# Four operations of the later phases moved: a v load to ScalarE's queue, a split unit by a slot, a weight table by a product, sums and split steps by one place

## The chip, the cores and the metric

One core of a Trainium2 chip runs the kernel. The metric is the device time of one execution in microseconds, the median over runs. TensorE (PE) multiplies, VectorE (DVE), ScalarE (ACT) and GpSimd (POOL) do elementwise work, and SyncE (SP) issues most DMAs; ScalarE and GpSimd can issue DMAs from their own queues as well. Each engine works through its instructions in the order in which the program gives them.

## What is computed

```python
# attention, per batch and head (4, 8, 768, 64), with 16 clusters
q_assign = argmax(normalized(q) @ normalized(centroids).T)      # and k_assign
scores = (q @ k.T) / 8, -1e9 where q_assign != k_assign
attn = softmax(scores);  y = attn @ v
# then, with the heads side by side: x is 3072 x 512
h = x @ w_in                     # 512 x 2048
g = h if h > 0 else exp(h) - 1
out = g @ w_out                  # 2048 x 512
```

## The kernel before

The kernel has three phases on one core, each a long stream for PE. All orders are written out by hand: an operation stands at the place in the program where it should come on its engine.

**Attention** runs in 32 slots, one per batch, half of the queries and pair of heads. A slot multiplies k by q for six key tiles (lines 540 and 553, the second is the cluster mask), ScalarE exponentiates each tile (line 576), and one slot later PE multiplies by v (line 596, `values`), ScalarE takes the result (line 610, `take_values`). In `told_and_values` v of slot n + 1 is asked for (`load_v`, line 195), in a buffer that the values of slot n - 1 have just left; in the slots of `second_of_pair` (3, 5, ..., 15) this stands behind the six key tiles, in the others ahead. q and k come in small pieces (line 181, sixteen loads for one half of the queries). Between the tiles the slots convert weights (lines 344 to 374, with a power step on ScalarE at line 354) and split pieces of w_in into rounded parts for the last phase: `split_here` asks for a unit's store (line 1026), `split_after` runs its two ScalarE operations at the end of the slot (lines 1019 and 1033), and the next slot's `split_here` stores the result (line 1043) and adds by a DMA of GpSimd (line 1044). The slots that may start a unit are `split_slots`.

**The first 1024 tokens** go through w_in (`first_pair`, line 1276) and then through w_out by a recursion in which seven products of half size replace eight, twice over. The outer seven (`UNITS`, M1 to M7) each have a quadrant or sum of w_out (a11, a12, a22, s1 to s4) and of g. The inner seven of a unit (`chain`, m1 to m7) need sums of that quadrant, its "table" (s2, s3, s4): `table_last` makes a22's (two ScalarE copies, line 997, and GpSimd's accumulating DMAs, line 999), `table_block` s4's in four VectorE steps (lines 930, 932, 935, 937), called one by one as `next(fourth)`. Tables are stored to DRAM (`keep_far`, line 914), and later groups of tokens fetch them back piece by piece (`fetch`, line 1079) into slots that come free. Within `chain`, ScalarE copies banks (lines 1534, 1571, 1592), VectorE adds (1578, 1595), makes the next unit's t1 to t4 (`t_step`, lines 1622 to 1628), and takes the quarters of the unit before into the output (`take`, line 1654). `taken` closes a unit: for M6 two sums of 128x512 on VectorE (line 1673), for M5 and M4 the stores of two output tiles each by SP (line 1682), for the others nothing. Output tiles of the second group of tokens use the places of the first, so their first sums must wait for those stores. `note` marks the places within a unit at which side work stands.

**The other 2048 tokens** go through w_in in two parts of 28 products (`k_phase`, lines 1345, 1393, 1355), with x split into three rounded parts (`x_split`: steps 0 and 2 on ScalarE at lines 1019 and 1139, steps 1 and 3 on VectorE at 1137 and 1141) at products given by `SPLIT_AT`, and after each part through w_out by two more runs of `chain`. After every product ScalarE copies its bank (line 1393), PE adds the third part on the copy, and VectorE adds to the result (line 1355).

Of the kernel before, what the change touches and what calls it, by code (L numbers as in the profile page):

```python
# [61 lines left out]
def main_path(ctx, tc, c, q, k, v, centroids, moe_w_in, moe_w_out, out):  # L62
# [131 lines left out]

    def load_v(n):
        b, _, pr = blocks[n]
        nc.sync.dma_start(
            v_raw[n % 2].rearrange("p h t d -> p h (t d)"),
            v[b, 2 * pr : 2 * pr + 2].rearrange("h (p t) d -> p h (t d)", t=NT),
        )  # L200
# [789 lines left out]
    def table_last(a, at, n):  # L990

        q11, q12, q21, q22 = (part_w(a, i, j) for i in range(2) for j in range(2))
        s3, s2, s4 = at
        minus = [(s2, q11)] if n == 0 else [(s3, s2), (s4, s2)]
        more = [(q21, q22), (s2, q21)] if n == 0 else [(s3, q22), (s4, q12)]
        for to, x in minus:
            nc.scalar.activation(to, x, Act.Copy, scale=-1.0)
        for to, x in more:
            nc.gpsimd.dma_start(to, x, accum_op=Alu.add)
        if n == 1:  # L1000
            parts = [("s3", s3), ("s2", s2), ("s4", s4)]
            here[a].update(parts)
            made.extend((flat_far(a, x), y) for x, y in parts)
# [44 lines left out]

    to_split = [(a, u) for a in ("a11", "a12", "a22", "s1") for u in range(4)]
    last_piece = {"a11": 1, "a12": 3, "a22": 7, "s1": 7}  # L1050
    split_slots = (9, 13, 15, 17, 21, 23, *range(3 * NB, 4 * NB))

    def split_here(n):
        while in_hand:
# [263 lines left out]
    def late_elu(step, n, e):  # L1318
        x = late_part(n)
        if n > 3:  # L1320
            x, e = in_columns(x), in_columns(e)
        relu_of_exp(step, x, e)

    def k_phase(part):

        pool = bank_pool("doubles")
        d = [pool.tile([P, 2, 512], F32, name=f"double{n}") for n in range(4)]
        bank_a, bank_b = [d[1], d[0]], [d[2], d[3]]
        c11, c21, c12, c22 = s_of
        into = (c21, c11, c21, c12, c21, c21, c12)  # L1330
        plus = (None, c21, c21, c21, c21, c21, c12)
        x11, x21, t2, t1, x12, _, x22 = k_operands(part)
        def minus(to, x, y):
            nc.vector.tensor_tensor(to, x, y, op=Alu.subtract)

        begin = 28 * part
        at = of_unit

        def times(n, bank, parts, first):
            i, u = divmod(n, 4)  # L1340
            w, x = w_ring[(begin + n) % 3], xh[(7 * part + i) % 2]
            for j in range(2):
                for ch in range(2):
                    for m in parts:
                        nc.tensor.matmul(  # L1345
                            bank[:, j],
                            lhsT=w[:, m, QS * ch + P * j : QS * ch + P * j + P],
                            rhs=x[m][:, ch],
                            start=first and ch == 0 and m == parts[0],
                            stop=ch == 1 and m == parts[-1],  # L1350
                            skip_group_check=True,
                        )

        def add(to, x, y):
            nc.vector.tensor_tensor(to, x, y, op=Alu.add)  # L1355

        on_act, on_dve = ({n: [] for n in range(29)} for _ in range(2))

        def plan(of, n, what, *args):
            of[n].append(lambda: what(*args))  # L1360

        for i in range(6):
            if i == 0 and part:
                continue
            q = 7 * part + i + 1
            for what, (of, n) in enumerate(zip((on_act, on_dve, on_act, on_dve), SPLIT_AT[i])):
                plan(of, n, x_split, q, what)
        for n, x in zip(
            ((0, 1, 3, 6), (0, 1, 2, 3))[part],
            ((t1, x12, x11), (t2, x22, t1), (x12, x22, x12), (x21, x21, t2)),  # L1370
        ):
            plan(on_dve, n, minus, *x)
        for c_, exps, ends in ((c11, (7, 7, 10, 14), (9, 11, 13, 15)), (c21, (23, 24, 26, 27), (25, 26, 27, 28))):
            for u in range(4):
                plan(on_act, exps[u], k_exp, at(c_, u), u)
                if ends[u] < 28:
                    plan(on_dve, ends[u], k_elu, at(c_, u), u)
        for u, n in ((0, 21), (3, 23)):
            plan(on_dve, n, add, at(c22, u), at(c22, u), at(c12, u))
        for t in ("t1", "t2"):  # L1380
            plan(on_dve, 24, t_step, 2 + 2 * part, 0, t, t_first)

        for n in range(29):
            if n < 28:
                i, u = divmod(n, 4)
                a, b = bank_a[n % 2], bank_b[n % 2]
                times(n, a, (0, 1), True)
                if begin + n + 3 < 56:
                    k_load(begin + n + 3, (0, 1))
            for what in on_act[n]:  # L1390
                what()
            if n < 28:
                nc.scalar.activation(at(into[0], u) if n < 2 else b, a, Act.Copy, scale=K_OF)  # L1393
            for what in on_dve[n]:
                what()
            if n > 0:
                m = n - 1
                i, u = divmod(m, 4)
                b, to = bank_b[m % 2], at(into[i], u)
                times(m, b, (2,), m < 2)  # L1400
                if begin + m + 3 < 56:
                    k_load(begin + m + 3, (2,))
                if m < 2:
                    add(to, b, to)
                elif plus[i] is None:
                    nc.scalar.copy(to, b)
                else:
                    add(to, b, at(plus[i], u))
                    if i == 4 and u in (1, 2):
                        add(at(c22, u), b, at(c12, u))  # L1410
                    elif i == 4:
                        nc.scalar.copy(at(c22, u), b)
            if part == 0 and 24 <= n < 28:
                if n == 24:
                    until[0] = len(streamed)
                    slots[:] = [xT[:, ch, GS * x : GS * x + GS] for x in (2, 3) for ch in range(KC)]
                fetch()
                fetch()
        k_elu(at(c21, 3), 3)
        for t in ("t3", "t4"):  # L1420
            t_step(2 + 2 * part, 0, t, t_first)

    SPLIT_AT = [(0, 2, 3, 4)]
    SPLIT_AT += [(4 * n, 4 * n, 4 * n + 1, m) for n, m in ((1, 5), (2, 10), (3, 14), (4, 17), (5, 22))]

    def first_elu(x, e):
        nc.vector.scalar_tensor_tensor(x, e, -1.0, x, op0=Alu.mult, op1=Alu.max)
# [1 line left out]
    class OutUnit:  # L1429
# [27 lines left out]
        def note(self, at):  # L1457
            k_, n = self.k_, self.n
            if k_ == 0:
                if (n, at) == (3, "m2"):  # L1460
                    next(first_table, None)
                if at in ("m2", "m7") and n in (3, 4):
                    g_step(k_, 5 - n, at == "m7")
                if (n, at) == (3, "m4"):
                    late_elu(2, 5, k_e[1])
                    table_last("a22", last, 1)
                elif (n, at) == (5, "m6"):
                    verdict_told()
                if (n, at) in ((4, "m4"), (5, "m6"), (5, "m2"), (5, "m7")):
                    next(fourth)  # L1470
                if (n, at) == (5, "m2"):
                    slots[:] = [*words_of, *thirds(x_sum)]
                    for _ in range(4):
                        fetch()
                elif (n, at) == (5, "m4"):
                    keep_far()
                    for _ in range(3):
                        fetch()
                elif (n, at) == (6, "m7"):
                    slots[:] = slots + beside[:3]  # L1480
                    for _ in range(3):
                        fetch()
                return
            if k_ == 1:
                ahead_of_k(n, at)
            for step, x in ELU_STEPS[1 if k_ == 1 else 2 + k_ % 2].get((n, at), ()):
                late_elu(step, x, dead_e[x % 2] if k_ == 1 else k_e[x % 2])
            if (n, at) in G_STEPS:
                g_step(k_, *G_STEPS[n, at])
            if k_ == 3 and (n, at) in SPLIT_AHEAD:  # L1490
                x_split(*SPLIT_AHEAD[n, at])
# [68 lines left out]
    def chain(units):  # L1560
# [5 lines left out]
        for i, u in enumerate(units):  # L1566
# [5 lines left out]
            if i > 0:  # L1572
                for q_ in (2, 3):
                    units[i - 1].take(q_)
                units[i - 1].taken()
            if nxt:
                nxt.t("t1")
            nc.vector.tensor_tensor(b2, b2, u.m5, op=Alu.add)
            if nxt:
                nxt.t("t2")  # L1580
            u.note("m6")
# [512 lines left out]
```

## Time and profile before

| | us |
|---|---|
| runs | 850.65, 851.0, 858.26 (median 851.0) |
| profiled execution | 852.49 |
| its span, first to last instruction | 850.7 |
| PE busy | 838.0 |
| VectorE busy | 756.3 |
| ScalarE busy | 509.6 |
| GpSimd busy | 120.6 |

In the profile a row of a timeline gives its start, its length, the engine and line, and in brackets how long the engine idled before it and what ended that idle time. A releaser is inferred; where the engine named was long done, another one, often a DMA, was the last.

### The profile page before, as it was taken

What the parts mean: (1) busy time and instruction counts of PE and PEld (TensorE: products, weight loads), DVE (VectorE), ACT (ScalarE), POOL (GpSimd) and SP (SyncE); (2) the same over time, 40 slices, a digit from 0 to 9 for tenths busy, and PEclk for the clock granted to TensorE, in tenths of its full rate; (3) what the DMA queues carried; (4) which work ended last, traced back from release to release, by engine and by line L of the source; (5) the groups of instructions that cost most, each with busy time, mean ns of one, the idle gap of its engine ahead of it and who ended that gap; (6) DMA issues with size and microseconds to landing.
All of it is one profiled execution on the core that took longest, in us unless ns stands there. A gap on an engine that the chain in (4) does not pass through costs nothing.

```text
span 850.7 us, 15122 instructions
## 1 busy us (share of the span) xinstructions
PE 838.0 (99%) x5584; PEld 585.7 (69%) x5584; DVE 756.3 (89%) x993; ACT 509.6 (60%) x827; POOL 120.6 (14%) x139
## 2 busy tenths in 40 slices
PE   9999999999999999999999999999999999999997
PEld 5444444444444444444698998888999988789997
DVE  7899999999997988987899887889999859899995
ACT  6887777887878875543722326765543266655521
POOL 0023131312224324121011000102000001020000
PEclk9999999999999999999999999999999999999999
DMA  8786796789659997899389968999867798847683
GB/s 176 162 211 185 161 229 162 184 187 232 149 140 278 323 262 204 252 269 299 100 164 239 305 209 288 288 292 323 253 212 227 214 292 289 285 133 236 206 239 117
DMA packets 184577, 190.91 MB, mean 224 GB/s; under 512 B 97584, under 2 KB 131376, under 8 KB 183472
## 3 DMA queue, kind: packets, MB, share of 16 engines
q1 hardware_dynamic: 174688, 163.32, 64.7%
q0 software_dynamic: 8688, 25.17, 14.5%
q10 hardware_dynamic: 1120, 1.38, 0.6%
q8 instruction: 46, 0.75, 0.4%
q14 instruction: 35, 0.29, 0.1%
HBM read 130.06 MB, written 51.38 MB: 213 GB/s over the span
## 4 chain that ended last, share of the span: by engine, by line
PE 83%; DVE 7%; DMA 4%; ACT 3%; issue 2%; SPq 0%; POOL 0%; ACTq 0%; DVEq 0%; POOLq 0%
PE bank L1099 28%; PE double L1345 15%; PE banks L1276 11%; PE banks L540 11%; PE o_bank L596 9%; PE banks L553 3%; PE d_bank L596 3%; PE d_bank L616 1%; DMA k_a<-spare 1%; DMA kq_g<-in_v_dram 1%; PE banks L454 1%; ACT p_out L576 1%; DMA ring<-k_s 1%; DVE sums_w L580 1%; DMA out_dram<-p_out 1%
## 5 line engine op out<-in xcount | busy, mean ns | idle before, releaser
L576 ACT ACTIVATE p_out<-banks 128x768 f32<-128x768 f32 x150 | 118.4, 813 | 9.2 <-PE banks L540 6.7
L596 PE MATMUL o_bank<-p_out,kq_g 128*64 128x384 f32 x600 | 102.3, 490 | 0.4 <-DMA kq_g<-in_v_dram 0.4
L596 PEld LDWEIGHTS o_bank<-p_out,kq_g 128*64 128x64 f32 x600 | 40.8, 137 | 59.6 <-issue 54.4
L1099 PE MATMUL bank<-xT 128*128 128x128 f32 x640 | 80.6, 275 | 0.0
L1393 ACT ACTIVATE double<-double 128x1024 f32<-128x1024 f32 x52 | 52.3, 1009 | 42.6 <-PE double L1345 26.4
L1099 PEld LDWEIGHTS bank<-xT 128*128 128x128 f32 x640 | 76.0, 192 | 0.0
L1145 POOL TENSOR_SCALAR k_e<-k_e 128x1024 f32<-128x1024 f32 x16 | 18.6, 1163 | 282.6 <-ACT k_e L1144 282.6
L1276 PE MATMUL banks<-xT,w_in 128*128 128x512 f32 x128 | 55.6, 594 | 0.0
L1355 DVE TENSOR_TENSOR kq_g<-double,kq_g 128x1024 f32<-128x1024 f32 x36 | 44.0, 1222 | 12.8 <-PE double L1345 10.3
L580 DVE TENSOR_TENSOR sums_w<-p_out 128x1536 f32<-128x1536 f32 x25 | 46.2, 1848 | 9.0 <-ACT p_out L576 8.9
L1571 ACT COPY bank<-bank 128x128 f32<-128x128 f32 x39 | 9.8, 251 | 67.9 <-PE bank L1099 67.9
L583 DVE TENSOR_TENSOR sums_w<-sums_w,p_out 128x1536 f32<-128x1536 f32 x25 | 44.3, 1772 | 1.8
L1276 PEld LDWEIGHTS banks<-xT,w_in 128*128 128x128 f32 x128 | 24.2, 190 | 30.9 <-issue 30.2
L1345 PE MATMUL double<-xh0h,ring 128*128 128x512 f32 x112 | 43.9, 392 | 0.3 <-ACT double L1393 0.2
L654 POOL TENSOR_TENSOR xT<-xT,sums_b 128x384 f32<-128x384 f32 x32 | 43.0, 1358 | 6.7 <-DMA sums_b<-xT 4.6
L1345 PE MATMUL double<-xh1h,ring 128*128 128x512 f32 x112 | 43.7, 390 | 0.0
L1345 PE MATMUL double<-xh0l,ring 128*128 128x512 f32 x112 | 43.6, 389 | 0.0
L1345 PE MATMUL double<-xh1l,ring 128*128 128x512 f32 x112 | 43.6, 389 | 0.0
L1099 PE MATMUL bank<-w_out,xT 128*128 128x128 f32 x288 | 38.4, 276 | 1.2 <-DVE xT L1622 1.2
L540 PE MATMUL banks<-x_sum,xT 64*128 64x384 f32 x192 | 38.2, 486 | 0.8 <-ACT p_out L576 0.7
L540 PE MATMUL banks<-kq_g 64*128 64x384 f32 x192 | 37.6, 483 | 0.8 <-ACT p_out L576 0.8
L540 PE MATMUL banks<-kq_g,xT 64*128 64x384 f32 x192 | 37.6, 483 | 0.0
(335 smaller groups left out, 2023.7 us busy)
## 6 DMA issues: line engine op xcount, KB each, us to landing
ring<-k_s SPq DMA_DIRECT2D x32, 512.0 KB, 4.7
xT<-far_s_s SPq DMA_DIRECT2D x63, 256.0 KB, 3.3
kq_g<-in_v_dram SPq DMA_DIRECT2D x32, 384.0 KB, 5.5
ring<-k_a SPq DMA_DIRECT2D x23, 512.0 KB, 4.9
xT<-far_s_q SPq DMA_DIRECT2D x38, 256.0 KB, 3.1
xT<-far_a_s SPq DMA_DIRECT2D x37, 256.0 KB, 3.2
ring<-k_s SPq DMA_DIRECT2D x32, 256.0 KB, 4.5
k_a<-w_in SPq DMA_DIRECT2D x24, 256.0 KB, 7.6
```

The source lines that it names most:

```text
L540: nc.tensor.matmul(s[:, e, :HS], lhsT=kT[b % 2][pr][rows, ts(kt, P)], rhs=qT[half][pr][rows], start=first, stop=not first,)
L553: nc.tensor.matmul(s[:, e, :HS], lhsT=hot_k[b % 2][rows, side, ts(kt, P)], rhs=q_mask[half][rows, side, pr % 2], start=first, stop=not first,)
L576: nc.scalar.activation(probs(n, kt), s[:, :, :HS], Act.Exp, scale=SCALE)
L580: nc.vector.tensor_tensor(add_four, p[0], p[1], op=Alu.add)
L583: nc.vector.tensor_tensor(add_four, add_four, four(n)[2], op=Alu.add)
L596: nc.tensor.matmul(value_bank(n)[64 * e : 64 * e + 64, :HS], lhsT=v_raw[n % 2][:, e, kt], rhs=probs(n, kt)[:, e], start=(kt == 0), stop=(k ...
L654: nc.gpsimd.tensor_tensor(x_of(n), x_of(n), r, op=Alu.mult)
L1099: nc.tensor.matmul(bank[:, :P], lhsT=left[:, f], rhs=right[:, f], start=first and f == 0, stop=last and f == 3, skip_group_check=True,)
L1276: nc.tensor.matmul(bank[:, j], lhsT=w[a][:, ch, QS * u + P * j : QS * u + P * j + P], rhs=x[:, ch], start=ch == 0, stop=ch == 1,)
L1345: nc.tensor.matmul(bank[:, j], lhsT=w[:, m, QS * ch + P * j : QS * ch + P * j + P], rhs=x[m][:, ch], start=first and ch == 0 and m == part ...
L1355: nc.vector.tensor_tensor(to, x, y, op=Alu.add)
L1393: nc.scalar.activation(at(into[0], u) if n < 2 else b, a, Act.Copy, scale=K_OF)
```

## The change

- `load_v`: for slot 4 alone ScalarE's queue issues the load, in place of SP's.
- `split_slots`: 17 becomes 18.
- `k_phase`: the second of two sums of c22 that VectorE makes on its own comes at product 22 in place of 23; the last split of a part has its steps 2 and 3 at products 22 and 23 in place of 21 and 22.
- `note`: in the first group of tokens, the second half of `table_last("a22")` comes behind m2 of unit 4 in place of m4 of unit 3; the four steps of the s4 table come behind m2, m7, m4 of unit 5 and m6 of unit 6, in place of m4 of unit 4 and m6, m2, m7 of unit 5; `keep_far` and three fetches that followed m4 of unit 5 follow m6 of unit 6.
- `chain`: `taken` of the unit before comes behind t1 and the sum of m5 into the bank, in place of ahead of both.

```diff
     def load_v(n):
         b, _, pr = blocks[n]
-        nc.sync.dma_start(
+        by = nc.scalar if n == 4 else nc.sync
+        by.dma_start(
...
-    split_slots = (9, 13, 15, 17, 21, 23, *range(3 * NB, 4 * NB))
+    split_slots = (9, 13, 15, 18, 21, 23, *range(3 * NB, 4 * NB))
...
-        for u, n in ((0, 21), (3, 23)):
+        for u, n in ((0, 21), (3, 22)):
             plan(on_dve, n, add, at(c22, u), at(c22, u), at(c12, u))
...
-    SPLIT_AT += [(4 * n, 4 * n, 4 * n + 1, m) for n, m in ((1, 5), (2, 10), (3, 14), (4, 17), (5, 22))]
+    SPLIT_AT += [(4 * n, 4 * n, 4 * n + 1, m) for n, m in ((1, 5), (2, 10), (3, 14), (4, 17))]
+    SPLIT_AT += [(20, 20, 22, 23)]
...
                 if (n, at) == (3, "m4"):
                     late_elu(2, 5, k_e[1])
+                elif (n, at) == (4, "m2"):
                     table_last("a22", last, 1)
                 elif (n, at) == (5, "m6"):
                     verdict_told()
-                if (n, at) in ((4, "m4"), (5, "m6"), (5, "m2"), (5, "m7")):
+                if (n, at) in ((5, "m2"), (5, "m7"), (5, "m4"), (6, "m6")):
                     next(fourth)
...
-                elif (n, at) == (5, "m4"):
+                elif (n, at) == (6, "m6"):
                     keep_far()
                     for _ in range(3):
                         fetch()
...
                 for q_ in (2, 3):
                     units[i - 1].take(q_)
-                units[i - 1].taken()
             if nxt:
                 nxt.t("t1")
             nc.vector.tensor_tensor(b2, b2, u.m5, op=Alu.add)
+            if i > 0:
+                units[i - 1].taken()
             if nxt:
                 nxt.t("t2")
```

## Rows read from the trace of the kernel before

**Rows 1.** The page's first part: busy us, share of the span, instructions.
```profile
PE 838.0 (99%) x5584; PEld 585.7 (69%) x5584; DVE 756.3 (89%) x993; ACT 509.6 (60%) x827; POOL 120.6 (14%) x139
```

**Rows 2.** Timeline of PE, where it idled: start, us, operation, idle before.
```profile
62.71 4.09 PE L596 MATMUL o_bank<-p_out,kq_g 128*64 128x384 f32 x24 [0.44 <-DMA kq_g<-in_v_dram]
...
189.23 0.92 PE L540 MATMUL banks<-x_sum,xT 64*128 64x384 f32 x4 [0.69 <-ACT p_out L576]
...
452.70 1.16 PE L1099 MATMUL bank<-x_sum,xT 128*128 128x128 f32 x8 [1.20 <-ACT bank L1571]
...
460.62 1.16 PE L1099 MATMUL bank<-w_out,xT 128*128 128x128 f32 x8 [0.51 <-DVE xT L1622]
...
672.42 1.16 PE L1099 MATMUL bank<-w_out,xT 128*128 128x128 f32 x8 [0.67 <-DVE xT L1622]
...
741.94 1.20 PE L1345 MATMUL double<-xh0m,ring 128*128 128x512 f32 x4 [0.44 <-ACT double L1393]
```

**Rows 3.** Timeline of SP's DMA issues, 38 to 66 us.
```profile
39.04 11.33 SPq L181 DMA_DIRECT2D w_out<-in_q_dram  x16
...
53.62 1.10 SPq L197 DMA_DIRECT2D kq_g<-in_v_dram  x2
```

**Rows 4.** Timeline of ScalarE, 38 to 66 us.
```profile
46.58 0.49 ACT L610 ACTIVATE xT<-o_bank 128x384 f32<-128x384 f32 x1 [2.11 <-PE o_bank L596]
...
50.45 0.49 ACT L610 ACTIVATE xT<-d_bank 128x384 f32<-128x384 f32 x1 [0.36 <-PE d_bank L596]
51.37 4.84 ACT L576 ACTIVATE p_out<-banks 128x768 f32<-128x768 f32 x6 [0.42 <-PE banks L540]
```

**Rows 5.** Line 197, the v loads: us from issue to landing, all 32.
```profile
DMA to landing us min/median/max: 3.1/5.5/13.8
```

**Rows 6.** Timeline of ScalarE, 182 to 198 us, slots 17 to 19.
```profile
185.78 0.61 ACT L1019 ACTIVATE w_out<-w_in 128x512 fp32r<-128x512 f32 x1
...
188.38 4.40 ACT L576 ACTIVATE p_out<-banks 128x768 f32<-128x768 f32 x6
...
196.77 0.49 ACT L610 ACTIVATE xT<-o_bank 128x384 f32<-128x384 f32 x1 [1.52 <-PE o_bank L596]
```

**Rows 7.** Timeline of SP's DMA issues, 440 to 476 us.
```profile
440.20 1.14 SPq L914 DMA_DIRECT2D far_s_s<-sums_b  x1
...
470.42 0.33 SPq L1079 DMA_DIRECT2D x_sum<-far_s_q  x1
...
475.32 0.90 SPq L1682 DMA_DIRECT2D out_dram<-p_out  x2
```

**Rows 8.** DMA issues around 440, 470 and 475: count, KB, us to landing.
```profile
far_s_s<-sums_b SPq DMA_DIRECT2D x1, 256.0 KB, 11.0
...
x_sum<-far_s_q SPq DMA_DIRECT2D x1, 256.0 KB, 2.6
...
out_dram<-p_out SPq DMA_DIRECT2D x1, 256.0 KB, 5.9
```

**Rows 9.** Timeline of ScalarE, around 451 and 573 us.
```profile
451.33 0.63 ACT L997 ACTIVATE sums_b<-p_out 128x512 f32<-128x512 f32 x1 [3.10 <-DVE xT L1622]
...
572.92 1.06 ACT L1139 ACTIVATE xh0l<-xh0l 128x1024 fp32r<-128x1024 f32 x1
```

**Rows 10.** Timeline of VectorE, 458 to 482 us.
```profile
458.67 1.29 DVE L1673 TENSOR_TENSOR sums_w<-sums_w 128x512 f32<-128x512 f32 x2
...
464.06 0.67 DVE L937 TENSOR_TENSOR xT<-sums_b,xT 128x512 f32<-128x512 f32 x1
...
467.85 0.27 DVE L1654 TENSOR_TENSOR p_out<-bank,sums_w 128x128 f32<-128x128 f32 x1
...
481.30 0.29 DVE L1654 TENSOR_TENSOR p_out<-bank,sums_w 128x128 f32<-128x128 f32 x1 [0.67 <-DMA out_dram<-p_out]
```

**Rows 11.** The chain that ended last, in order of time: start, us, work.
```profile
486.51 21.72 PE bank L1099 x192
```

**Rows 12.** Waits of PE from 560 to 580 us: total, times, longest.
```profile
PE double L1345 <- ACT double L1393: 0.4, 1, 0.4
```

## The prediction

> **What bounds the kernel now.** I read the page's first part first: TensorE (PE) is busy 838.0 us, 99% of the span [rows 1]. What the change can win is PE's idle time, 850.7 - 838.0 = 12.7 us in all. The timeline of PE comes next, for the places where an idle stands with a releaser [rows 2]: each is a single late operation, with PE busy for many microseconds on both sides. So each edit is costed at its own place, from the timelines of the engines there, and then asked what is late next.
>
> **v of slot 4 by ScalarE's queue.** At 62.71 PE has been idle 0.44 us for v [rows 2]. SyncE's queue shows why v is late: it is free when ScalarE takes the values of slot 2 at 46.58 [rows 4], but SP is in a string of sixteen q loads from 39.04 on (11.33 us), then k loads, and reaches v at 53.62 [rows 3]. ScalarE would issue it behind that take, at about 47.1. Over all v loads the landing took 3.1 to 13.8 us [rows 5], so it lands between 50.2 and 60.9, before PE comes at 62.3: gain 0.44. The price is ScalarE's own issue; two v loads took SP 1.10 [rows 3], so 0.55. Queued behind it on ScalarE are the copies and masks of the next q half, the take at 50.45 and the exponentials from 51.37 on; these two had idled 0.36 and 0.42 for PE, 0.78 of cover [rows 4]. Without it the edit would cost 0.55. SP's later loads, v of slot 5 first, go that much earlier. Bounds: gain 0.44, loss 0.55; I take the gain, since the cover is measured right behind.
> The Trainium skill speaks against this edit: by "DMA: Bandwidth & Descriptors", section "Issuing engines are not separate DMA queues", all issuers share the same 16 DMA engines, and a second one saves only the time to issue, usually small. Here the string ahead of v on SP is exactly issue time, and it is not small; the transfer itself I leave at its rows. By the page alone the edit would win about nothing and the sum be 0.4 smaller.
>
> **Split unit from slot 17 to 18.** At 189.23 PE has waited 0.69 for an exponential [rows 2]. Ahead of the exponentials (188.38) stand, on ScalarE, copies and masks, the split unit's two operations (0.61 at 185.78 and one like it, 1.2 together) and the power step [rows 6]. Without the 1.2 the exponentials begin as soon as the scores are there: gain 0.69. One slot later the pair falls behind slot 18's exponentials, and the take at 196.77 had idled 1.52 for PE [rows 6]: that hides 1.2, with 0.3 to spare. Without this cover the 0.69 comes back there. The unit's two SP issues move behind the k and weight loads of slot 18, ahead of a v load that is used a slot later; its end (an SP store and GpSimd's accumulating DMA) moves to slot 19, on a queue whose engine is busy 14% of the span [rows 1]. Bounds: 0.69 or nothing; I take 0.69.
>
> **The a22 table, the s4 table, and M6's sums.** The idle of 1.20 at 452.70 is for ScalarE's copy for m7 [rows 2], which stands behind the a22 table's two operations, of 0.63 each; the first starts at 451.33 after an idle of 3.10 [rows 9]. The label names a VectorE step; but the store of that part of sums_b, issued at 440.20 [rows 7], took 11.0 to land [rows 8], at 451.2. ScalarE waits for that DMA, which the edit doesn't touch. What it changes is who stands behind: one product later the copy for m7 goes first, and behind the pair is now the copy for the next unit, whose user is four products on. Gain 1.20, and VectorE, which waits for the same copy, comes 1.2 earlier too. At 460.62 PE has waited 0.51 for t1 [rows 2], which stands behind M6's two sums (1.29) [rows 10] and a step of the s4 table; both now follow it: gain 0.51. Together 1.71.
> But the gain has to pass the stretch from 464 to 487. The last s4 step (VectorE, ends at 464.73) moves behind the work up to 467.85, 3.1 us of it [rows 10]. With VectorE 1.2 earlier it ends at 464.73 - 1.2 + 3.1 = 466.6, 1.9 later than before. SP then stores the table's pieces and fetches one back: that fetch, which must wait until the piece has landed, went at 470.42 [rows 7], 5.7 behind the step; now at 472.3. SP's queue from there to the store of the first output tiles at 475.32 took 4.90; the other output store (two issues, 0.90 as at 475.32) now goes ahead of the s4 pieces, so 4.0 remain [rows 7], and the store leaves at 476.3 instead of 475.32. Its landing took 5.9; a fetch on an empty queue took 2.6 [rows 8]. So it lands between 478.9 and 482.2; I take 5.1, near the row of the store itself, less a little for the other store that no longer stands ahead: 481.4. VectorE's next output sum waits for exactly this store, until 481.30 before [rows 10], and behind it stand VectorE's steps up to the t1 that releases PE at 486.51 [rows 11]. So VectorE resumes 0.1 later than before, however early PE comes: of the 1.71 nothing is left. Bounds: gain 1.71 (landing in 2.6), loss 0.9 (5.9).
> The fetched piece lands at 472.3 + 2.6 = 474.9, before its first product, so no wait there.
>
> **ScalarE's and VectorE's steps of the third phase.** In each of its two parts PE waits 0.44 for ScalarE's copy of product 21: 741.94 is one [rows 2], the wait of 560 to 580 the other [rows 12]. Ahead of that copy stands the split step at 572.92 (1.06), itself late because it waits for VectorE [rows 9]. One product later it follows the copy, which begins up to 0.96 earlier and covers 0.44: twice, 0.88. The split's last step changes places on VectorE with a c22 sum of the same size; the users are products 24 and later, two products on. Without that slack the 0.44 comes back. Bounds: 0.88 or nothing; I take 0.88.
>
> **M6's sums later, in the fourth unit group.** At 672.42 PE has waited 0.67 for t1 [rows 2], again behind the two sums, 1.29 as at 458.67 [rows 10]. They now follow t1 and the bank sum, and t2 ends when it did. Bounds: 0.67 or nothing; I take 0.65, since VectorE has split steps of its own there and PE comes close behind it. In the other groups PE shows no idle at this place, so nothing.
>
> **The sum.** 0.44 + 0.69 - 0.1 + 0.88 + 0.65 = 2.56 us. The profiled execution took 852.49 (span 850.7, the rest outside it), 1.5 above the median of the three runs. The gain lies inside the span, 850.7 - 2.6 = 848.1, so the profiled time would be 849.9; off the median it is 851.0 - 2.6 = 848.4.
>
> **The rivals.**
> *The tables' gain is kept.* For it: if the output store lands in 2.6, at 478.9, it is there about when VectorE comes (481.30 less its idle of 0.67 and the 1.7), and PE keeps 1.71. Against it: the same store took 5.9 behind the same fetches. Time: 851.0 - (0.44 + 0.69 + 1.71 + 0.88 + 0.67) = 846.6.
> The Trainium skill, same page, section "Anatomy of one DMA", has a fixed part of about 2.0 us plus bytes over 436 GB/s: an estimate of 2.6 for 256 KB. The lone fetch agrees (2.6), the store doesn't (5.9); by the page alone this rival's time would be the forecast.
> *Slower: the s4 pieces land late.* With a longer line of stores a landing took 11.0 [rows 8], where the sum has at most 5.7. With 11.0 SP's fetch goes at 466.6 + 11.0 = 477.6, the output store leaves at 481.6 and lands 5.1 to 5.9 later, at about 487.1, 5.8 behind before, and PE with it: 851.0 - 2.66 + 5.8 = 854.1. It decides from a fetch at about 474.9 on, where its loss of 2.66 has eaten the other edits' gain. Against it: the s4 pieces come after a pause of stores, as before.
> *The waits only move.* Each removed idle comes back at the next narrow place, the attention's in a later slot, the third phase's at a later copy. For it: VectorE is close behind PE in every stretch read. Against it: after each idle of rows 2 PE ran on without one. Time: 851.0.
>
> **How the numbers follow.** Forecast 0.5, tables' gain kept 0.3, waits move 0.1, slower 0.1. The forecast's own range, its tables between a gain of 0.9 and the loss of 0.9 and one small edit failing, is 847.4 to 850.1. The range 846.0 to 851.6 takes in the gain kept and the waits moved, and leaves out the slower case and part of the spread of the runs (850.65 to 858.26). About 1%, 8.5 us, is what a measurement of this kernel can tell from no change. No case here reaches that by itself; the slower one could, with a longer landing or an unlucky median. So faster by over 1% 0.02, within 1% 0.95, slower by over 1% 0.03.
>
> **What would show it.** Right: the idles of rows 2 are gone from PE's timeline; SP's store of the first output tiles leaves some 1 us after 475.32, counted from the end of the first phase, and VectorE waits 2 us or more for its landing instead of 0.67. If that wait stays under 1 us, the tables' gain is kept. If the s4 fetch comes 4 us later than before, the slower rival holds. If PE waits for ScalarE in slot 4 or 19, the first two edits were priced wrong; and a new idle of PE behind product 22 or 24 would refute the third phase's.

## The result, and the profile after

The changed kernel takes 862.1 us (median of eight executions between 859.7 and 863.2) against 851.1 for the kernel before, measured side by side: a ratio of 1.012 (95% interval 1.010 to 1.014). One of the eight executions of the kernel before took 4941 us and moves neither figure. The change costs 11 us; the forecast was 848.4, and all of its range lay below 852.

The profiled execution took 862.7 us, its span is 860.9. First part of the page of the kernel after (busy us, share of the span, instructions), to be read against [rows 1]:

```profile
PE 841.3 (98%) x5584; PEld 587.4 (68%) x5584; DVE 754.7 (88%) x993; ACT 509.7 (59%) x827; POOL 124.6 (14%) x139
```

PE's idle time has grown from 12.7 to 860.9 - 841.3 = 19.6 us, and PE has become 3.3 us busier on the same 5584 matmuls. The longest waits of PE over the whole span of the kernel after (releaser, total, times, longest):

```profile
PE banks L455 <- DVE x_sum L842: 5.3, 1, 5.3
PE banks L455 <- DVE kq_g L833: 3.8, 1, 3.8
PE bank L1100 <- DVE p_out L1626: 1.7, 1, 1.7
PE banks L541 <- ACT p_out L577: 1.2, 1, 1.2
```

Two idle times are new and large, released by VectorE's transposes of q (x_sum) and of k (kq_g). PE's timeline of the kernel after shows where they are, and what followed:

```profile
66.86 1.51 PE L455 MATMUL banks<-x_sum,cT 128*32 128x384 f32 x8 [5.25 <-DVE x_sum L842]
...
73.43 1.49 PE L455 MATMUL banks<-kq_g,cT 128*32 128x384 f32 x2 [3.79 <-DVE kq_g L833]
74.85 5.59 PE L597 MATMUL o_bank<-p_out,kq_g 128*64 128x384 f32 x24
```

This is slot 4, the place of the one v load that was moved. The last row answers to the first of [rows 2]: its wait of 0.44 for v is gone, as forecast, but the row starts 12.1 us later (0.6 of this the execution lags from its first matmul on), and its 24 matmuls take 5.59 us where they took 4.09. The windows of the kernel after (stretch, length, busy PE PEld DVE ACT POOL, then PE's granted clock, DMA share, GB/s) show why they take longer:

```profile
40.00:60.00 20.00, 20.00 (x146) 9.68 (x144) 11.31 (x16) 17.04 (x25) 4.40 (x7) 1.00 0.59 149
60.00:80.00 20.00, 10.96 (x56) 3.28 (x54) 14.76 (x19) 4.20 (x8) 0.00 (x0) 0.66 0.66 135
80.00:100.00 20.00, 20.00 (x144) 9.48 (x142) 19.58 (x23) 16.45 (x24) 6.75 (x5) 1.00 0.46 151
```

Behind the idle times the granted clock is at its lower level (1.2 GHz) for a while, 0.66 in the mean of that stretch. All other edits work later, and the start of the same matmul in both traces shows what they did: it is 13.4 us later than before at 169 us and 9.4 us later at 742 us. So they win some 4 us, and the v load alone loses about 13, the lag of 0.6 taken off.

**What delayed q and k.** VectorE's timeline and SP's issues, kernel after, 38 to 70 us:

```profile
64.93 1.78 DVE L842 STREAM_TRANSPOSE x_sum<-w_out 128x1536 f32<-128x1536 f32 x1 [11.95 <-DMA w_out<-in_q_dram]
```
```profile
39.32 18.62 SPq L181 DMA_DIRECT2D w_out<-in_q_dram  x16
58.05 6.89 SPq L181 DMA_DIRECT2D w_out<-in_k_dram  x4
```

VectorE stands still for 11.95 us for a q load, and then works without a pause up to k's transpose at 72.40, which ends PE's second idle time. SP's sixteen q loads took 11.33 us to issue in [rows 3]; now they take 18.62. The waits of SP's queue in this stretch name a transfer that is not on that queue at all:

```profile
SPq L181 <- DMA kq_g<-in_v_dram: 6.8, 1, 6.8
```

The instruction list of the built kernel says how SP comes to wait for ScalarE's load. Each DMA of SP's and ScalarE's queues reports its landing on one of eight semaphores, DMAHW0 to 7, handed out in turn over both queues, and before it is issued it waits until the DMA that had the same one before has landed. In the order of the program, with what each waits for:

```
SP   DMA w_out<-in_k_dram   [waits DMAHW7]
ACT  DMA kq_g<-in_v_dram    [waits DMAHW7, DMAHW0]
SP   DMA w_out<-in_k_dram   [waits DMAHW1]        the last k load of slot 2
SP   DMA w_out<-in_q_dram   [waits DMAHW2, DVE]   the first q load
...
SP   DMA w_out<-in_q_dram   [waits DMAHW7]
SP   DMA w_out<-in_q_dram   [waits DMAHW0]        the seventh q load
```

v(4) took the turn of DMAHW0 ahead of the last k load of slot 2. So the seventh of the sixteen q loads, eight turns on, waits for v to land, and v is issued only when ScalarE has got through its stream. The chain that ended last in the kernel after, 36 to 84 us, runs through exactly this:

```profile
47.27 3.32 DMA kq_g<-in_v_dram
50.60 0.58 SPq L181
...
57.30 7.56 DMA w_out<-in_q_dram
...
64.93 1.79 DVE x_sum L842
```

One more thing can be read there: the wait ends at 50.60, but the last q load then takes 7.56 us to land. The experiments below had to say how much of the 13 us is the wait and how much the landing.

### The profile page after: what moved, and what is told of

Its sections match the earlier page's. It is cut to its first block, busy times and chain, and to the rows that moved or that the text cites. A ratio compares the mean times of both kernels' runs of the same rounds, so it can differ in the third digit from the quotient of the medians.

```text
span 860.9 us, 15119 instructions
## 1 busy us (share of the span) xinstructions
PE 841.3 (98%) x5584; PEld 587.4 (68%) x5584; DVE 754.7 (88%) x993; ACT 509.7 (59%) x827; POOL 124.6 (14%) x139
## 4 chain that ended last, share of the span: by engine, by line
PE 85%; DMA 6%; DVE 5%; SPq 2%; ACT 1%; issue 1%; DVEq 0%; ACTq 0%; POOLq 0%
PE bank L1100 26%; PE double L1346 17%; PE banks L541 12%; PE banks L1277 11%; PE o_bank L597 10%; PE banks L554 3%; PE d_bank L597 3%; DMA k_a<-w_in 2%; PE d_bank L617 1%; DMA w_out<-in_q_dram 1%; SPq L181 1%; DMA k_a<-spare 1%; PE banks L455 1%; DMA ring<-k_s 1%; DMA out_dram<-p_out 1%
## 5 line engine op out<-in xcount | busy, mean ns | idle before, releaser
L1356 DVE TENSOR_TENSOR kq_g<-double,kq_g 128x1024 f32<-128x1024 f32 x36 | 44.0, 1221 | 12.1 <-PE double L1346 10.7
L655 POOL TENSOR_TENSOR xT<-xT,sums_b 128x384 f32<-128x384 f32 x32 | 45.1, 1427 | 5.4 <-DMA sums_b<-xT 3.8
L660 POOL DMA_DIRECT2D sums_b<-xT x28 | 17.9, 658 | 160.5 <-DVE xT L634 109.7
```

The source lines that it names most:

```text
L655: nc.gpsimd.tensor_tensor(x_of(n), x_of(n), r, op=Alu.mult)
```

## The experiments

The edits are shown by their main lines, `...` marks what is left out, and `v(4)` is the v load of slot 4.

**Which edit.** The first theory was the turn of the semaphores; its rivals were the order and sharing of the transfers (v's 384 KB ahead of q and k), and a loss that several edits make together. v(4) back on SP's queue, all else as changed:

```diff
-        by = nc.scalar if n == 4 else nc.sync
+        by = nc.sync
```

> The changed kernel with v of slot 4 back on SP's queue, all else as changed. Theory (turns): the loss of the changed kernel comes from this one load. Eight landing semaphores go round over the DMAs of SP's and ScalarE's queues; v took one ahead of a string of q loads that SP issues long before ScalarE gets to v, and the eighth DMA after it must wait for v's landing (SP 6.8 us, then PE 5.25 and 3.79 idle and half clock). Then this kernel keeps only the other edits' gain: PE idles 0.4 again near 62, and by the shifts read from the two traces behind that place (13.6 us late at 78 us, 9.6 late at the end) it is 4.0 faster than before: about 847, between 846 and 849. Rival (something in the other edits costs too, for instance the new idles near 295 and 487): 850 or more.

Measured: 851.2 us, ratio to the kernel before 0.998 (0.996 to 1.000). The 11 us are gone. But the 847 expected was missed: the other edits win 1.0 here and not 4. Two places where the rest goes show in PE's waits from 55 to 80 us and in its timeline in this kernel:

```profile
PE o_bank L597 <- DMA kq_g<-in_v_dram: 2.4, 1, 2.4
```
```profile
486.81 1.16 PE L1100 MATMUL bank<-words_w,p_out 128*128 128x128 f32 x8 [1.95 <-DVE p_out L1626]
```

PE waits 2.4 us for v(4) where it waited 0.44, and behind the 1.95 at 487 us the clock falls to its lower level, which in the kernel after it does not; both are taken up below. And the kernel before with that one edit alone:

```diff
-        nc.sync.dma_start(
+        by = nc.scalar if n == 4 else nc.sync
+        by.dma_start(
...
```

> The kernel before with this edit alone: v of slot 4 by ScalarE's queue. Theory (turns): PE idles 5.3 and 3.8 near 66 and 73 us at half clock, and the run takes 851 + 13 = about 864, between 862 and 866. Rival (the loss needs the other edits as well): 851 or less.

Measured: 867.2 us, ratio 1.018 (1.016 to 1.020), 1 us above the range expected; in the profiled execution, the fastest of the five at 863.4, PE has the same two waits, 5.0 and 3.8, and SP the same one. The edit alone carries the loss.

**The turn, or v's bytes.** First v(4) by a queue that has no part in these turns, GpSimd's (its DMAs report on other semaphores in the instruction list), in the changed kernel:

```diff
-        by = nc.scalar if n == 4 else nc.sync
+        by = nc.gpsimd if n == 4 else nc.sync
```

> The changed kernel with v of slot 4 asked for by GpSimd's queue, whose DMAs do not take turns with those of SP and ScalarE. v comes as early as with ScalarE and shares the DMA engines with the same q loads. Theory (turns): no wait of SP of several us in the q string, no idle of PE near 62 to 75, about 846.6 (847 less the 0.4 wait for v). Rival (v, coming early, takes bandwidth or order from the q loads): SP's string is as late as in the changed kernel and the time stays near 860.

Measured: 853.2 us, ratio 1.001 (0.999 to 1.003). SP's wait is gone, and most of the loss. But not all, and the 846.6 expected was missed: PE idles once. Waits of PE in the kernel with v(4) by GpSimd, 55 to 80 us:

```profile
PE banks L455 <- DVE kq_g L833: 3.7, 1, 3.7
```

So something in the transfers counts too. To part the two, a small piece of v through ScalarE's queue, which takes the same turn but moves 24 KB early in place of 384:

```diff
+        if n == 4:
+            nc.scalar.dma_start(to[:8], src[:8])
+            nc.sync.dma_start(to[8:], src[8:])
+            return
...
```

> The kernel before, with only 8 of the 128 partitions of v(4) (24 KB of 384) asked for by ScalarE's queue and the other 120 by SP's, where v(4) always was. The small piece takes the same turn among the landing semaphores as the whole v(4) did in the changed kernel. Theory of the turns: SP's seventh q load still waits until ScalarE has issued the piece at about 47 us and it has landed, 2 to 2.5 us later; SP waits 5 to 6.5 us there, the transposes of q and k come late, and the kernel takes 861 to 867 us. Rival (the early 384 KB of v take the place of q and k in the transfers): with 24 KB moved early nothing is late, 850.5 to 852.5.

Measured: 864.7 us, ratio 1.014 (1.011 to 1.018). The bytes of v are not needed for the loss; the turn is. SP's waits in this kernel, 36 to 70 us, and VectorE's stall:

```profile
SPq L181 <- DMA kq_g<-in_v_dram: 5.2, 1, 5.2
```
```profile
64.70 1.78 DVE L844 STREAM_TRANSPOSE x_sum<-w_out 128x1536 f32<-128x1536 f32 x1 [11.64 <-DMA w_out<-in_q_dram]
```

Then the whole v(4) by ScalarE six turns and about 6 us later, so that the thirteenth q load is the one that waits:

```diff
             exponential(n, kt, s)
+            if (n, kt) == (4, 2):
+                load_v(4)
...
```

> The kernel before, with v(4) by ScalarE's queue, but behind the third exponential of slot 4 instead of ahead of slot 4; its turn is then six DMAs later, so that the thirteenth q load and not the seventh is the one with the same semaphore. Theory of the turns: SP stops at the thirteenth, from about 47.5 us until v, issued at about 53.5, has landed at about 56.5 to 57; then 4 q and 4 k loads follow; SP's wait is 8 to 10 us, k is asked for at 59 to 60 us (58.05 in the changed kernel), and the kernel takes 861 to 868 us, no better than with the early place (867.2). Rival (v's bytes ahead of q and k): v asked for 6 us later, behind twelve q loads, costs less than the early place, 851 to 857 us.

Measured: 866.2 us, ratio 1.017 (1.013 to 1.020): no better, as the theory of the turns had it, although v goes behind twelve of the q loads. Its wait was missed by a little: SP waited 7.1 us, not 8 to 10, and k was asked for at 59.57.

**Why 5.2, 6.8 and 7.1 us of waiting cost about the same.** In the kernels of these three runs (the small piece, v alone, v later) VectorE's stall ends at 64.70, 64.43 and 64.33. Something else ends it. The DMA issues of the kernel after tell what (count, KB, median us to landing): first those of 50.5 to 54.2 us, then those of 54.53 to 57.9.

```profile
w_out<-in_q_dram SPq DMA_DIRECT2D x6, 48.0 KB, 2.5
```
```profile
w_out<-in_moe_w_in_dram POOLq DMA_DIRECT2D x1, 1024.0 KB, 6.0
spare<-in_moe_w_in_dram POOLq DMA_DIRECT2D x1, 1024.0 KB, 9.5
w_out<-in_q_dram SPq DMA_DIRECT2D x4, 48.0 KB, 8.9
```

At 54.27 and 54.83 GpSimd's queue asks for two pieces of w_in of 1 MB each. The six q loads ahead of them landed in 2.5 us, the four behind them in 8.9, at 63.6 to 64.9, about when the second megabyte was in (54.83 + 9.5 = 64.3). SP's wait made the string late; being overtaken by the two large loads would make it later still. To measure this part by itself, the changed kernel with seven extra multiplications on GpSimd ahead of the two loads:

```diff
                 places.extend(next_places)
...
+                for _ in range(7):
+                    nc.gpsimd.tensor_tensor(spare_w[:, :HS], x_of(0), r_of, op=Alu.mult)
                 ask(nc.gpsimd)
```

> The changed kernel, unaltered but for seven extra multiplications on GpSimd (0.98 us each, into a buffer that is overwritten next) ahead of its two 1 MB table loads, which so are asked for at about 61 us instead of 54.27 and 54.83. In the changed kernel SP's wait of 6.8 us pushed the last four q loads and all k loads behind these two loads, and they landed only after 63.5 us. Theory (half of the loss is the wait itself, half is being overtaken by the tables): SP still waits 6 to 7 us for v, but the last q piece lands at 59.5 to 61 us instead of 64.9, VectorE and TensorE come 6 to 8 us late instead of 12 to 13, and the kernel takes 855 to 858.5 us. Rival (the wait for the turn alone sets the loss, whoever transfers): 861 to 863.5, as the changed kernel.

Measured: 857.0 us, ratio 1.005 (1.004 to 1.007). The seven took 8.32 us, so the large loads went at 61.88. SP still waited 6.1, but VectorE's stall halved. VectorE's and PE's timelines in this kernel:

```profile
58.16 1.78 DVE L845 STREAM_TRANSPOSE x_sum<-w_out 128x1536 f32<-128x1536 f32 x1 [5.86 <-DMA w_out<-in_q_dram]
```
```profile
67.49 1.49 PE L455 MATMUL banks<-kq_g,cT 128*32 128x384 f32 x2 [5.28 <-DVE kq_g L836]
68.90 5.96 PE L597 MATMUL o_bank<-p_out,kq_g 128*64 128x384 f32 x24
```

Against the same matmuls of the kernel before, PE comes to the 24 matmuls with v 6.3 us late, not 11.5 (12.1 less the lag of 0.6), and leaves them 8.1 us late, not 13. So of the 13 us the wait for the turn makes some 6, being overtaken some 5 more, and the lower clock on the 24 matmuls about 1.5. These are one profiled execution each; the medians, 862.1 and 857.0, differ by the same 5.

The same reading fits what v by GpSimd kept: there v came ahead of the q loads' tail, the last two k loads left SP at 54.09 and 54.72, just behind the large loads (53.97, 54.54), and landed in 10.6 us. And it fits the 0.44 for v in [rows 2] that the edit was to remove. In the profiled executions with v(4) on SP's queue, v took the longer to land, the shorter its lead on the first of the two loads was (one execution each):

| kernel | v(4) left, against the first megabyte | us to landing |
|---|---|---|
| a22 steps alone | 0.86 ahead | 3.7 |
| s4 steps alone | 0.36 ahead | 4.3 |
| split unit, third phase, sums | 0.24 ahead | 6.3 |
| before | 0.04 ahead | 9.1 |
| v(4) on SP, stores on GpSimd | 0.02 ahead | 11.0 |
| v(4) on SP, s4 steps back | 0.01 behind | 10.3 |
| v(4) on SP | 0.15 behind | 10.9 |

The kernels of this table that have not been met yet follow below. To test the reading, v(4) goes by GpSimd right ahead of the two loads, with the s4 steps at their old places:

```diff
                 places.extend(next_places)
+                load_v(4)
                 ask(nc.gpsimd)
...
```

> The version with the s4 steps and v(4) at the old places (848.4 us), and v(4) issued by GpSimd's queue right in front of the two 1 MB tables of M6. In that version SP issued v at 53.94 us and GpSimd the tables at 53.93, and TensorE waited 1.7 us for v; in the kernel before v led by 0.1 us and the wait was 0.44. Theory (v lands late when the tables are asked for first): v lands ahead of them, the wait at 62 us is under 0.3 us, and the median is 846.3 to 847.3. Rival (all transfers share the stretch of 50 to 60 us, whoever is first): the k loads or the tables land later instead, TensorE or VectorE waits for them 1 us or more, 848 to 850.

Measured: 848.25 us, ratio 0.996 (0.994 to 0.998). v of slots 4 and 5 landed in 4.6 and 3.8 us and PE has no wait in slot 4 any more, where the same kernel with v(4) on SP waited 1.7. The total is not better for it: between 63 and 140 us PE loses 1.4 us against that kernel, 0.7 of it in two waits for exponentials; the rest of this loss was not settled. The expectation of 846.3 to 847.3 was missed.

**The give-back at 487 us.** The prediction had the table moves win 1.71 us and lose it all where an output store gets late behind the later s4 steps. With the s4 steps and their fetches back at the old places, v(4) on SP, all other edits kept:

```diff
-                if (n, at) in ((5, "m2"), (5, "m7"), (5, "m4"), (6, "m6")):
+                if (n, at) in ((4, "m4"), (5, "m6"), (5, "m2"), (5, "m7")):
                     next(fourth)
...
-                elif (n, at) == (6, "m6"):
+                elif (n, at) == (5, "m4"):
                     keep_far()
```

> As the first of this call (v on SP), and the s4 table's four steps, its stores and the three fetches back at their old places; a22's second half and M6's sums stay moved. Theory (the tables' gain of 2.2 at 453 and 461 is given back at 487 because the later s4 steps push SP's fetch and the store of the first output tiles back): SP's fetch of the s4 piece goes at least 1.5 us earlier against the work around it, VectorE waits less for the store, and PE's idle of 1.7 near 487 shrinks to under 0.8; time 0.5 to 1.5 under the first of this call. Rival (the idle is VectorE's own load): the idle stays at 1.5 or more and the time is the same.

Measured: 848.4 us, ratio 0.995 (0.993 to 0.997), faster than both kernels and by more than expected against v(4) on SP (2.8 us, not 0.5 to 1.5). PE gives nothing back at 487 us, but 0.6 at 466. Waits of PE from 464 to 468 us in this kernel:

```profile
PE bank L1100 <- DVE p_out L1626: 0.7, 1, 0.7
```

The same from the other side, v(4) on SP and the s4 steps late, but two output stores by GpSimd's queue:

```diff
-            store_tile(k_, 2 * tiles + i, nc.sync)
+            store_tile(k_, 2 * tiles + i, nc.gpsimd if (k_, tiles) == (0, 0) else nc.sync)
```

> The changed kernel with v(4) back on SP's queue, and the first two output stores of M4 (two of 256 KB) issued by GpSimd's queue instead of SP's. Without the last edit it took 851.2 us and gave back 1.9 us at 486.5 us, where VectorE waited 2.55 us for an output store that SP had issued at 476.15 us, after nine fetches, and 1.6 us more at half clock right behind. Theory (the later s4 steps put SP's fetches ahead of the store, and the store lands late): off SP's string the store leaves early, VectorE's wait at 481 us is under 0.7 us, the shift against the kernel before stays near -1.6 us at 486.5 us, and the median is 847.5 to 849. Rival (VectorE's own order or the shared transfers set that wait, not SP's string): wait of 1.5 us or more stays, 850.5 to 852.

Measured: 848.0 us, ratio 0.994 (0.992 to 0.996). The store leaves at 469.74 and not at 476.15, and VectorE's wait for it is gone. Waits of VectorE from 470 to 490 us, first with v(4) on SP alone (the store behind the fetches), then the wait of PE that is left in the kernel with the stores on GpSimd's queue:

```profile
DVE p_out L1658 <- DMA out_dram<-p_out: 2.5, 1, 2.5
```
```profile
PE bank L1100 <- DMA x_sum<-far_s_q: 1.2, 1, 1.2
```

The second one is new: PE waits 1.2 for a fetch that left at 472.29 and landed at 478.11, behind the stores.

**The edits one by one**, on the kernel before. The a22 table's steps alone:

```diff
                 if (n, at) == (3, "m4"):
                     late_elu(2, 5, k_e[1])
+                elif (n, at) == (4, "m2"):
                     table_last("a22", last, 1)
```

> The kernel before with the move of a22's table steps alone. Theory: this move alone takes the idle times of 1.20 us at 452.70 us and 0.51 us at 460.62 us away, gives 0.64 us back at 466 us, and leaves SP's output store where it was: net 1.6 us, 849.2 to 850.2 us. Rival (the s4 steps at their old place were what held ScalarE or VectorE there): both idle times stay, 850.7 to 851.7.

Measured: 850.85 us, ratio 0.998 (0.996 to 1.000). The 1.20 at 452.70 is gone, PE is 1.5 us earlier there. But the 0.51 at 460.62 stays, as 0.49; that part of the theory was wrong, and the time lies above the range expected. The s4 steps and their fetches alone:

```diff
-                if (n, at) in ((4, "m4"), (5, "m6"), (5, "m2"), (5, "m7")):
+                if (n, at) in ((5, "m2"), (5, "m7"), (5, "m4"), (6, "m6")):
...
```

> The kernel before with the move of the s4 steps and of their SP fetches alone. Theory: nothing is won at 452.70 and 460.62 us (1.20 and 0.51 us idle stay); the output store stands behind the fetches, VectorE waits 2 to 3 us for it at 481 us, TensorE 1.5 to 2 us behind it and 1 to 1.6 us more at the lower clock: slower by 1.5 to 3.5 us, 852.5 to 855 us. Rival (the move brings part of the gain at 440 to 470 us): 849.5 to 851.5.

Measured: 855.7 us, ratio 1.005 (1.003 to 1.007), a little above the range expected. They take the idle at 460.62 away (0.6) and cost far more behind it. PE's timeline and its windows in this kernel:

```profile
487.74 1.60 PE L1099 MATMUL bank<-words_w,p_out 128*128 128x128 f32 x8 [1.84 <-DVE p_out L1622]
```
```profile
484.00:486.00 2.00, 1.90 (x18) 1.71 (x16) 2.00 (x4) 0.27 (x1) 0.00 (x0) 1.00 1.05 398
486.00:488.00 2.00, 0.26 (x2) 0.26 (x3) 2.00 (x7) 0.43 (x2) 0.00 (x0) 1.00 1.05 382
488.00:490.00 2.00, 2.00 (x13) 2.00 (x13) 2.00 (x3) 0.27 (x1) 0.00 (x0) 0.57 0.69 248
```

An idle of 1.84 us, and behind it the granted clock falls to the lower level for some 3 us, which costs 1.6 more. It is not always so: with v(4) by GpSimd's queue PE idles 1.80 us at the same place, and the clock stays up. PE's timeline and its window there:

```profile
489.99 1.16 PE L1100 MATMUL bank<-words_w,p_out 128*128 128x128 f32 x8 [1.80 <-DVE p_out L1626]
```
```profile
490.00:492.00 2.00, 2.00 (x18) 2.00 (x19) 2.00 (x4) 0.27 (x1) 0.00 (x0) 1.00 0.66 244
```

The rest, the split unit, the third phase and M6's sums:

```diff
-    split_slots = (9, 13, 15, 17, 21, 23, *range(3 * NB, 4 * NB))
+    split_slots = (9, 13, 15, 18, 21, 23, *range(3 * NB, 4 * NB))
...
+    SPLIT_AT += [(20, 20, 22, 23)]
...
-                units[i - 1].taken()
...
+            if i > 0:
+                units[i - 1].taken()
```

> The kernel before with the split unit in slot 18, the third phase's check later and M6's sums a product earlier; v(4), the tables' steps of a22 and s4 as before. Theory: each of these removes its own idle time (0.7 to 1 us at 189 us, 0.8 at 575, 1.0 at 672, 0.85 at 742), and they add up: faster by 2.5 to 4 us, 847 to 849 us. Rival (they only move waits): 850.5 to 851.5.

Measured: 849.1 us, ratio 0.997 (0.995 to 0.999). PE's waits from 540 to 760 us, the kernel before and then this one:

```profile
PE double L1345 <- ACT double L1393: 1.3, 4, 0.4
PE bank L1099 <- DVE xT L1622: 0.7, 1, 0.7
```
```profile
PE double L1346 <- DMA ring<-k_s: 0.7, 1, 0.7
PE double L1346 <- ACT double L1394: 0.2, 1, 0.2
```

The waits aimed at are all but gone. The 0.7 for a fetch is new; the kernel after does not have it.

Taken by the medians the parts give: a22 -1.2, s4 +3.6, the rest -2.9, together -0.4, where all of them in one kernel (v(4) on SP) gave -1.0. With the 15 of v alone this would make 14, and the changed kernel lost 11. Some of the difference is visible: in the changed kernel the idle of 1.72 at 498.75 was not followed by the lower clock. Of the four other kernels with late s4 steps and the stores on SP's queue three lost 1.6 to it (idle of 1.84, 1.95 and 1.95), and the one with 1.80 did not. The rest is within the intervals.

## Why the prediction was wrong, point by point

**v of slot 4: the step that failed.** Gain of 0.44 forecast, loss of 13 measured in its stretch. v's own way was as forecast: issued at 47.27 (forecast 47.1), landed at 50.59 (forecast 50.2 to 60.9), before PE wanted it. The price on ScalarE was smaller than the 0.55 put down. ScalarE's timeline around the issue, the kernel before and then after:

```profile
46.58 0.49 ACT L610 ACTIVATE xT<-o_bank 128x384 f32<-128x384 f32 x1 [2.11 <-PE o_bank L596]
47.08 1.03 ACT L483 COPY w_out<-w_out 64x384 bf16<-64x384 bf16 x2
```
```profile
47.21 0.49 ACT L611 ACTIVATE xT<-o_bank 128x384 f32<-128x384 f32 x1 [2.11 <-PE o_bank L597]
47.27 0.38 ACTq L198 DMA_DIRECT2D kq_g<-in_v_dram  x1
47.71 1.03 ACT L484 COPY w_out<-w_out 64x384 bf16<-64x384 bf16 x2
```

The issue ran beside the take, and the copies begin 0.50 us after the take's start in both; the idle times of 0.36 and 0.42, the prediction's cover, are still there and were not needed. The sentence that failed is "SP's later loads, v of slot 5 first, go that much earlier." In its place the runs show SP's seventh q load waiting 6.8 us for v's landing, and the string behind it late with it. The sentence took SP's queue to be independent of ScalarE's once v had left it. The sum asked who is queued behind v on ScalarE, and never who waits for v's landing on SP. The bounds had the same hole: gain 0.44, loss 0.55, both for the issue alone, where a wait between the queues had no term. Nor did any term see that the last q load left only 4.0 us and the last k load 0.8 us ahead of two large loads of GpSimd's, so that a delay of the string would be nearly doubled; [rows 3] ended at the v loads, and GpSimd's queue in that stretch was not read. The same queue bears on why v was late at all: the prediction laid it to the string ahead of v on SP, but v took 9.1 us to land with the large load 0.04 behind it, and 3.7 with a lead of 0.86. No rival had its place in slot 4 either.

The prediction weighed a rule of the Trainium skill here ("DMA: Bandwidth & Descriptors", section "Issuing engines are not separate DMA queues": the issuers share the 16 DMA engines, another issuer saves issuing time only). What the trace shows of sharing agrees: q loads of 48 KB took 2.5 us ahead of the large loads and 8.9 behind them. The forecast passed over that side of it.

**Split unit: right.** 0.69 forecast; the wait at 189.23 is gone and PE gains 0.96 there, in the kernel after and in the kernel with the split but without v alike. Nothing came back in slot 19. A wait near 305 us (0.81 in the kernel before, 1.15 after) is gone in other kernels, the one with v alone among them, which has no edit there; what sets it stays open.

**Tables: the mechanism right, some sizes off.** With v on SP the store left at 476.15 (forecast 476.3) and landed at 481.51 (481.4), and VectorE waited 2.55 for it instead of 0.67 in [rows 10] (forecast 2 or more). That the two times agree so well is in part luck: this execution already stood 0.6 us behind the kernel before at 440 us. Counted from there the store left 0.2 later than before, not 1.0; PE won 2.2 us up to 480 us (forecast 1.71) and gave back 1.9 of them by 487 (forecast all). So the give-back is as worked out, within half a microsecond. The estimate of 2.6 us that the prediction set beside its rows is from a formula that the Trainium skill ("DMA: Bandwidth & Descriptors", section "Anatomy of one DMA") gives for DMAs that GpSimd issues; the fetch and the store here are SP's. Not foreseen: that the idle of 1.84 or 1.95 us there can be followed by a stretch at the lower clock, 1.6 us more; so the s4 move is a clear loss. And the gain was put down too evenly: a22's steps alone bring the 1.20; the 0.51 goes with the s4 steps or with M6's sums, either alone. What the s4 move buys beside the sums is the wait of 0.7 at 466 us, which the kernel with the s4 steps back has and the one with v on SP has not.

**Third phase and M6's sums: right, a little small.** Forecast 0.88 and 0.65. PE's waits for ScalarE's copies fall from 1.3 to 0.2, and in the kernel after PE gains 0.7 at 575 us, 0.7 at 742 and 0.9 at 672.

**Size of the whole.** Without v the forecast gain was 2.1. Measured with v on SP it is 1.0 (851.2 against 852.2), where in the profiled execution PE waits 2.0 longer for v and the lower clock takes 1.6; with the s4 steps back too it is 3.9 (848.4). The reasoning held within a microsecond or two where it followed all queues of a stretch, and failed by 13 us where it followed one. The chance of 0.03 for a loss of over 1% came from having one slower case, the late s4 pieces, and none for the v load.

## What to carry to other kernels

When a DMA is moved to another engine's queue, look in the built kernel's instruction list for the semaphore it reports on and for the DMA that has it next: that one cannot leave before the moved one has landed, on SP's and ScalarE's queues alike, and a string in a hurry must not be the one. Before a load is delayed or advanced, list what every queue issues within a few microseconds of it: here loads of 48 KB took 2.5 us ahead of two of 1 MB and 8.9 behind them. And allow for more than its own length when an edit opens an idle of PE near 2 us: in three of the five kernels that had one of 1.72 to 1.95 at the same place, the lower clock took 1.6 us on top; behind one of 2.43 in slot 4 it did not.

## What the runs showed that was not expected

- A DMA on SP waited up to 7.1 us for the landing of one on ScalarE's queue with which it shares no data, only a turn among eight landing semaphores.
- A few tenths of a microsecond between two requests decide: v of 384 KB landed in 3.7 us when it left 0.86 us ahead of the first of two loads of 1 MB, in 6.3 when 0.24 ahead, and in 9.1 to 11.0 when 0.04 ahead or less; one profiled execution each.
- An idle of PE of 1.84 to 1.95 us was followed by some 3 us at the lower clock in three kernels; one of 1.72, one of 1.80 and, in slot 4 with v(4) on SP, one of 2.43 were not. These are one profiled execution each, and what decides stays open. Behind the two idle times of slot 4 the same 24 matmuls took 5.59 us instead of 4.09.
- The best kernels of the study (s4 steps back, or the stores on GpSimd's queue, v(4) not on ScalarE's) take 848.0 to 848.4 us, ratios 0.994 to 0.996; their intervals overlap, and which of them is best stays open.
